# Inverse root of the mean squares on Pool by the power operation, in place of logarithm and exponentials on ScalarE

## The chip, the core and the metric

The kernel runs on one core of a Trainium2 chip. Its time is the device time of that core in microseconds (us). Before the change the median of three runs is 384.19 us (383.76 to 384.19). In the profile the engines are called PE (TensorE matmul; PEld is its weight load), DVE (VectorE), ACT (ScalarE), POOL (GpSimd, called Pool in this text) and SP (SyncE, which only issues transfers here).

## The reference

Attention comes first, over 8 batches of 12 heads with 448 tokens of 64 values. Every row of q and k is divided by the root of its mean square and multiplied by a gain, then comes softmax attention. Its output is the input of a layer of 8 experts, to which the tokens go by a hash of their identity. The first part is what the change touches:

```python
def rmsnorm(x, g):
    rms = np.sqrt(np.mean(x * x, axis=-1, keepdims=True) + 1e-06)
    return x / rms * g
q_n, k_n = (rmsnorm(q, g_q), rmsnorm(k, g_k))
scores = scale * np.matmul(q_n, k_n.transpose(0, 1, 3, 2))
attn = exp(scores - max); attn = attn / sum(attn)
attn_out = np.matmul(attn, v)
# then, for each expert e: out[mask] = np.maximum(x[mask] @ w1[e], 0.0) @ w2[e]
```

## The kernel before

The kernel has two stages, one after the other. The attention stage takes roughly the first 185 us, the expert stage the rest. In both, the instructions of every engine run in the order in which the program writes them (`tc.manual_schedule()`): an instruction that has to wait holds up everything behind it on the same engine.

**Steps and groups.** A step is one pair of heads; there are 48, six for each batch b. Steps are gathered into 17 groups g0 to g16, of three pairs each, but for the first two (one and two pairs). `s0[g]` is the first step of a group. Scores, exponentials and the product with v are done step by step. The norm of q and k is prepared for a whole group at a time, about three steps ahead.

**One step.** `score(s, j)` (L490 to L504) makes a block of scores on PE and its exponential on ACT (L498, and L503 for the last, smaller block). `transposes(s+1)` brings normalized q and k of the next step into the layout that the matmul needs, on PE (L475), and `transposed` evacuates them on DVE (L485 for kT, L487 for qT). `av_part(s-1, ...)` multiplies the exponentials of the step before with v on PE; at its end DVE takes the reciprocal of the row sums (L535) and multiplies (L536).

**The norm of a group**, which the change touches, has four parts.
1. `prep_sq` squares q or k (DVE, L275).
2. `prep_sum` and `prep_red` sum them up, on PE by matmuls with the identity (L287) and on DVE by a reduction (L295). The result is `ss`, the sums of squares: 128 partitions with 24 values for q and 24 for k.
3. `prep_rr` (L298 to L311) makes from `ss` the inverse root `rr`, on ACT: one logarithm (L303, in place, with the division by 64 and the epsilon), and two exponentials with the factor -0.5 (L305), one for q and one for k. The exponentials write each value twice, side by side, as 16-bit floats.
4. `prep_norm` (L313 to L323) multiplies q and k by `rr` in four instructions on DVE (L320). The results are what `transposes` reads.

**Where these stand.** From g3 on, `prep_rr` of group g is written at the end of step t = s0[g-1], and `prep_norm` of g in the middle of step t+1. Between the last reduction (L295) of a group and its `prep_norm`, DVE has only the rest of step t and the start of step t+1: L535, L536, L485, L487, and in the table steps also two small instructions of the routing table (L442).

**Pool's order.** Pool issues nearly all loads: q, k and v of later batches (`load_qk` and `load_v`, L230 to L240) and the expert weights (L156 for w1, L162 for w2, L816 in the expert stage). A load can be made to wait until an earlier load has landed, and then holds Pool's queue. Pool also sets up constants, clears buffers (L577, L580, L581, L599), and in the middle of the attention stage does part of the routing (L365 to L439) and 28 instructions `hi` (L444) of the routing table. At the end of the attention stage it starts the gathers (L173).

Of the kernel before, what the change touches and what calls it, by code (L numbers as in the profile page):

```python
# [8 lines left out]
FP32 = mybir.dt.float32  # L9
# [3 lines left out]
AF = mybir.ActivationFunctionType  # L13
ALU = mybir.AluOpType
# [5 lines left out]
def kernel(  # L20
# [12 lines left out]
    nc = tc.nc  # L33

    B, H, S, D = q.shape
# [3 lines left out]
    P = 128  # L39
# [5 lines left out]
    scale = 1.0 / float(D) ** 0.5  # L45
# [26 lines left out]
    consts = ctx.enter_context(tc.tile_pool(name="consts", bufs=1))  # L72
# [9 lines left out]

    tid32 = rt_keep.tile([P, NTC, 2], I32)
    gcol = consts.tile([P, 2], FP32)
    ident16 = consts.tile([P, P], FP16)
    u128 = consts.tile([P, P], BF16)
    ones128 = consts.tile([P, P], BF16)
    eps_col = consts.tile([P, 1], FP32)
# [110 lines left out]
    with tc.manual_schedule(), \  # L199
# [98 lines left out]
        def prep_rr(gi):  # L298
            n = groups[gi][2]
            ss = st[gi].pop("ss")  # L300
            m = 8 * n
            rr = a_st.tile([P, 2, 2, GMAX, 4, 2], FP16, name="rr")
            nc.scalar.activation(ss[:, :, 0:m], ss[:, :, 0:m], AF.Ln, bias=eps_col[:], scale=1.0 / D)  # L303
            for a in range(2):
                nc.scalar.activation(  # L305
                    rr[:, a, :, 0:n].rearrange("p hh n j t -> p n hh j t"),
                    ss[:, a, 0:m].rearrange("p (n hh j) -> p n hh j", hh=2, j=4)[
                        :, :, :, :, None].to_broadcast([P, n, 2, 4, 2]),
                    AF.Exp, bias=0.0, scale=-0.5)
            st[gi]["rr"] = rr  # L310
            st[gi]["n8"] = a_n8.tile([P, 2, GMAX, 4, 2, D], FP16, name="n8")  # L311
# [264 lines left out]
        def zero_q(eng, t, n0, n1):  # L576
            eng.memset(t[64:P, n0:n1, 3::4, :], 0.0)  # L577

        def zero_kv(eng, t, n0, n1):
            eng.memset(t[64:P, n0:n1, 3, :], 0.0)  # L580
            eng.memset(t[0:64, n0:n1, 7, :], 0.0)  # L581
# [8 lines left out]
        zero_kv(nc.vector, first[:, 1], 0, 1)  # L590
        zero_q(nc.vector, first[:, 0], 0, 1)
        nc.vector.memset(eps_col[:], 1e-6)
        zero_kv(nc.vector, k_bufs[0], 0, HP)
        zero_q(nc.vector, q_bufs[0], 0, HP)
        zero_kv(nc.vector, v_bufs[0], 0, HP)
# [18 lines left out]
        for a in (1, 0):  # L614
            prep_sq(0, a)
            prep_sum(0, a)
            spin(2)
            prep_red(0, a)
        prep_rr(0)
        spin(6)  # L620
        prep_sq(1, 1, True)
# [15 lines left out]
        prep_red(1, 0)  # L637
        score(0, 0)
        prep_rr(1)
        for j in (1, 2, 3):  # L640
            score(0, j)
# [19 lines left out]
        for g in range(1, NG):  # L661
            t = s0[g - 1]
            if g > 1:
                pre[t].append((prep_v, g))
            else:
                pre[1].append((prep_v, g))
            if g > 3:
                pre[s0[g - 2]].append((prep_sq, g, 1))
                mid[s0[g - 2] + 1].append((g, 1))
                pre[t - 1].append((prep_sq, g, 0))  # L670
                mid[t].append((g, 0))
            if g == 2:
                pre[1].append((prep_sq, 2, 0))
                mid[1] += [(2, 1), (2, 0)]
                post[1] += [(prep_rr, 2), (prep_norm, 2)]
            if g == 3:
                pre[2].append((prep_sq, 3, 1))
                mid[3] += [(3, 1), (3, 0)]
                pre[3].append((prep_sq, 3, 0))
            if g > 2:  # L680
                post[t].append((prep_rr, g))
                pre[t + 1].append((prep_norm, g))
        for s in range(1, NS):
            gi, i = steps[s]
            b, hp0, n = groups[gi]
# [226 lines left out]
```

## Time and profile before

The profile is of one execution with a span of 385.0 us. The table gives busy time in us by engine in four stretches of the span; a stretch's length is the most that one engine can be busy in it.

| stretch, us | PE | DVE | ACT | Pool | what runs |
|---|---|---|---|---|---|
| 0 to 50 (50) | 36.82 | 32.57 | 28.55 | 39.91 | first loads, norms of groups g0 to g4 |
| 50 to 100 (50) | 45.96 | 45.26 | 45.88 | 17.51 | attention, loads of later batches |
| 100 to 160 (60) | 57.69 | 58.97 | 56.04 | 29.12 | attention with the routing table |
| 160 to 180 (20) | 18.90 | 17.44 | 18.29 | 1.36 | last attention steps |
| 180 to 385 (205) | 185.16 | 61.76 | 38.73 | 87.17 | experts |

In such a table the engine with the least idle time in a stretch is the first candidate for what bounds it. In the expert stage this is PE alone. In the attention stage three engines are nearly full at once, so the waits of single instructions have to be read as well.

A page of the profile names groups of instructions by line, engine and operation, with the count, the busy time, the mean time of one in ns, and the idle time of the engine just ahead of them with what ended it. The timeline lists instructions in order of time: start, duration, engine, line, operation, output and input; the bracket at its end holds idle time and what ended it.

### The profile page before, as it was taken

The numbers are of one execution on the slowest core, as the hardware profiler recorded it, in microseconds if no ns is written. First come the engines' busy times: TensorE is split into PE (matmuls) and PEld (weight loads), VectorE is DVE, ScalarE is ACT, GpSimd is POOL, SyncE is SP. The second block draws the span as 40 slices with busy tenths as digits, with TensorE's granted clock in tenths as the row PEclk, the third lists the DMA queues.
The fourth block names the chain that finished last, engine by engine and source line by source line (L and its number), as shares of the span: only waits on it lengthen the run. The fifth ranks groups of instructions, "written<-read, shape, count | busy, mean of one in ns | idle before, by whom it ended". The sixth has DMA issues, their size and how long they took to land. (4 is left out here: it accounts for less than half of the span.)

```text
span 385.0 us, 9539 instructions
## 1 busy us (share of the span) xinstructions
PE 344.5 (89%) x4006; PEld 236.8 (62%) x4006; DVE 216.0 (56%) x519; ACT 187.5 (49%) x299; POOL 175.1 (45%) x247
## 2 busy tenths in 40 slices
PE   7755998989999999999899999999998989999960
PEld 3443776766766777776667666666665656666630
DVE  5674789989999999988633233333222322232210
ACT  3753899989899999989321112212021111212200
POOL 8998552014629950003347344462644636522030
PEclk9998899999999999999999999999999999999995
DMA  8999999943999999103548999999999999932030
GB/s 123 159 131 181 189 220 193 219 61 76 191 185 234 218 242 198 44 15 105 122 116 159 212 260 247 205 257 174 236 233 194 239 186 235 269 138 95 2 147 2
DMA packets 54269, 64.61 MB, mean 168 GB/s; under 512 B 22403, under 2 KB 42134, under 8 KB 53968
## 3 DMA queue, kind: packets, MB, share of 16 engines
q0 software_dynamic: 50592, 57.98, 85.8%
q1 hardware_dynamic: 3024, 5.41, 5.2%
q8 instruction: 32, 0.52, 0.6%
q10 hardware_dynamic: 608, 0.59, 0.5%
q14 instruction: 13, 0.11, 0.1%
HBM read 89.68 MB, written 18.09 MB: 280 GB/s over the span
## 5 line engine op out<-in xcount | busy, mean ns | idle before, releaser
L498 ACT ACTIVATE expT<-sc_ps 128x896 bf16<-128x896 f32 x144 | 123.9, 934 | 22.7 <-PE sc_ps L496 22.5
L765 PE MATMUL o_ps<-w_sb,h_sb 128*128 128x256 f16 (+1 forms) x512 | 87.9, 326 | 0.0
L752 PEld LDWEIGHTS <-w_sb 128*128 128x128 f16 x432 | 58.0, 144 | 25.7 <-issue 1.6
L752 PE MATMUL h_ps<-xT,w_sb 128*128 128x512 f16 x336 | 73.7, 379 | 0.0
L765 PEld LDWEIGHTS <-h_sb 128*128 128x128 f16 x512 | 48.9, 98 | 32.6
L173 POOL DMA_INDIRECT xg<-x_scratch,gidx x32 | 32.6, 1020 | 63.5 <-DVE x_sb L536 38.3
L770 POOL DMA_INDIRECT out_dram<-o_sb,gidx x32 | 33.0, 1031 | 51.5 <-ACT o_sb L769 17.0
L756 ACT ACTIVATE h_sb<-h_ps 128x512 f16<-128x512 f32 (+2 forms) x36 | 19.7, 550 | 75.1 <-PE h_ps L752 75.1
L758 DVE TENSOR_SCALAR h_sb<-h_ps 128x512 f16<-128x512 f32 (+2 forms) x36 | 22.8, 632 | 55.6 <-PE h_ps L752 55.6
L769 ACT COPY o_sb<-o_ps 128x768 f32<-128x768 f32 x16 | 12.8, 799 | 76.0 <-PE o_ps L765 51.3
L520 PEld LDWEIGHTS <-expT 128*128 128x128 bf16 x1152 | 42.5, 98 | 9.9 <-issue 6.0
L496 PE MATMUL sc_ps<-qT,kT 64*128 64x448 f16 x288 | 43.3, 358 | 4.5 <-DVE et L385 1.4
L520 PE MATMUL av_ps<-v,expT 128*128 128x65 bf16 x1152 | 44.0, 194 | 0.0
L769 DVE COPY o_sb<-o_ps 128x768 f32<-128x768 f32 x16 | 15.3, 958 | 45.7 <-PE o_ps L765 21.2
L816 POOL DMA_DIRECT2D w_sb<-in_moe_w_dram x36 | 23.1, 645 | 30.2 <-DMA w_sb<-in_moe_w_dram 28.2
L475 PE MATMUL qkT_ps<-ident,n 128*128 128x128 f16 x384 | 30.6, 222 | 5.4 <-DVE n L320 3.8
L475 PEld LDWEIGHTS <-n 128*128 128x128 f16 x384 | 22.3, 98 | 19.8 <-issue 11.9
L536 DVE TENSOR_TENSOR x_sb<-av_ps,srec 128x448 f16<-128x448 f32 x48 | 29.7, 619 | 1.5
L287 PEld LDWEIGHTS <-ident 128*128 128x128 f16 x544 | 24.6, 99 | 8.8 <-issue 6.8
L185 DVE COPY xT<-xT_ps 128x768 f16<-128x768 f16 x28 | 15.5, 554 | 23.9 <-PE xT_ps L184 23.8
L485 DVE TENSOR_SCALAR kT<-qkT_ps,g_col 128x512 f16<-128x512 f16 x48 | 23.1, 481 | 9.5 <-PE qkT_ps L475 8.4
L503 ACT ACTIVATE expT<-sc_ps 128x448 bf16<-128x448 f32 x48 | 27.7, 577 | 1.2 <-PE sc_ps L501 1.2
(140 smaller groups left out, 382.5 us busy)
## 6 DMA issues: line engine op xcount, KB each, us to landing
w_sb<-in_moe_w_dram POOLq DMA_DIRECT2D x32, 384.0 KB, 13.6
w_sb<-in_moe_w_dram POOLq DMA_DIRECT2D x12, 768.0 KB, 13.5
x_scratch<-x_sb SPq DMA_DIRECT2D x15, 288.0 KB, 6.1
w_sb<-in_moe_w_dram POOLq DMA_DIRECT2D x2, 1536.0 KB, 16.4
kr<-in_k_dram POOLq DMA_DIRECT2D x6, 384.0 KB, 9.0
qr<-in_q_dram POOLq DMA_DIRECT2D x3, 768.0 KB, 14.5
vr<-in_v_dram POOLq DMA_DIRECT2D x6, 384.0 KB, 19.4
kr<-in_k_dram POOLq DMA_DIRECT2D x6, 288.0 KB, 8.9
```

The costliest lines, as they stand in the source:

```text
L173: nc.gpsimd.indirect_dma_start(out=xg[:], out_offset=None, in_=x_dram[0:rows, :], in_offset=bass.IndirectOffsetOnAxis(ap=idx, axis=0), bou ...
L287: nc.tensor.matmul(sp, lhsT=ident16[:], rhs=sq[:, c, 0:m], start=(c == 0), stop=(c == NW - 1))
L475: nc.tensor.transpose(T[:, o:o + P], n8[:, a, i, j].rearrange("p h d -> p (h d)"), ident16[:])
L496: nc.tensor.matmul(sc[:, hh, :S], lhsT=kT[64 * hh:64 * hh + 64, P * j:P * j + P], rhs=qT[64 * hh:64 * hh + 64, :], start=True, stop=True)
L498: nc.scalar.activation(expT[:, 2 * j:2 * j + 2, :], sc[:, :, :S], AF.Exp, bias=0.0, scale=1.0)
L503: nc.scalar.activation(expT[:, 6, :], sc[:, 0, :S], AF.Exp, bias=0.0, scale=1.0)
L520: nc.tensor.matmul(av[:, 2 * t + hh, :], lhsT=expT[:, tl(hh, j), P * t:P * t + P], rhs=v8[:, i, 4 * hh + j, 0:D + 1], start=(j == 0), stop ...
L536: nc.vector.tensor_tensor(out=x_sb[:, :, hp * D:hp * D + D], in0=av[:, :, :D], in1=srec[:, :, None].to_broadcast([P, SL, D]), op=ALU.mult)
L752: nc.tensor.matmul(h_ps[:, :c1 - c0], lhsT=w1v[:, co, fo, :], rhs=xT[:, co, c0:c1], start=(co == 0), stop=(co == CO - 1))
L765: nc.tensor.matmul(o_ps[:, d0:d1], lhsT=h_sb[:, fo, col * P:(col + 1) * P], rhs=w2_sb[:, fo, d0:d1], start=(fo == 0), stop=(fo == FO - 1))
L769: (nc.vector.tensor_copy if col % 2 else nc.scalar.copy)(o_sb[:], o_ps[:])
L770: scat = nc.gpsimd.indirect_dma_start(out=out[:, :], out_offset=bass.IndirectOffsetOnAxis(ap=idx, axis=0), in_=o_sb[:], in_offset=None, bo ...
```

## The change

From group g3 on (`gi > 2`), `prep_rr` is done by four instructions of Pool in place of three of ACT: a multiply and add for the mean and the epsilon, a power with the exponent -0.5, which is read from a new constant column `mhalf`, and two copies that write each value twice as 16-bit floats. Groups g0 to g2 keep the logarithm and the exponentials on ACT. The change is meant to take work from ACT, which also makes all exponentials of the softmax, and to put it on an engine with more idle time.

```diff
+    mhalf = consts.tile([P, 1], FP32)
...
-            nc.scalar.activation(ss[:, :, 0:m], ss[:, :, 0:m], AF.Ln, bias=eps_col[:], scale=1.0 / D)
+            on_pool = gi > 2
+            if on_pool:
+                nc.gpsimd.tensor_scalar(out=ss[:, :, 0:m], in0=ss[:, :, 0:m], scalar1=1.0 / D,
+                                        scalar2=1e-6, op0=ALU.mult, op1=ALU.add)
+                nc.gpsimd.tensor_tensor(out=ss[:, :, 0:m], in0=ss[:, :, 0:m],
+                                        in1=mhalf[:, :, None].to_broadcast([P, 2, m]), op=ALU.pow)
+            else:
+                nc.scalar.activation(ss[:, :, 0:m], ss[:, :, 0:m], AF.Ln, bias=eps_col[:],
+                                     scale=1.0 / D)
             for a in range(2):
+                if on_pool:
+                    nc.gpsimd.tensor_copy(
+                        rr[:, a, :, 0:n].rearrange("p hh n j t -> p n hh j t"),
+                        ss[:, a, 0:m].rearrange("p (n hh j) -> p n hh j", hh=2, j=4)[
+                            :, :, :, :, None].to_broadcast([P, n, 2, 4, 2]))
+                    continue
                 nc.scalar.activation(
                     rr[:, a, :, 0:n].rearrange("p hh n j t -> p n hh j t"),
...
         nc.vector.memset(eps_col[:], 1e-6)
+        nc.vector.memset(mhalf[:], -0.5)
```

## The prediction

> **What bounds the kernel now.** I read the page's table of slices first, to see which engine is full where.
>
> ```profile
> PE   7755998989999999999899999999998989999960
> DVE  5674789989999999988633233333222322232210
> ACT  3753899989899999989321112212021111212200
> POOL 8998552014629950003347344462644636522030
> ```
>
> The change acts only in the attention stage, slices 5 to 19. PE, DVE and ACT are all nearly full there, so no engine can simply be called the bound. The busy times by stretch separate them: from 100 to 160 us DVE is busy 58.97 of 60 us, ACT 56.04, PE 57.69; from 50 to 100 us DVE 45.26 of 50, ACT 45.88. So between 100 and 160 DVE is the bound and ACT has 4 us to spare; between 50 and 100 neither has much. From 180 us on PE is busy 185 of 205 us, and the expert stage can't start before the last scores: a delay of attention is a delay of the end.
>
> Next the groups that the change removes, kept apart by shape.
>
> ```profile
> L305 ACT ACTIVATE rr<-ss 128x48 f16<-128x48 f32 x30 | 5.6, 234 | 0.5
> L303 ACT ACTIVATE ss<-ss,eps_col 128x48 f32<-128x48 f32 x15 | 4.9, 326 | 0.1
> ```
>
> Then the timeline of DVE around one norm (g4), for the time that a replacement has.
>
> ```profile
> 48.74 0.25 DVE L295 TENSOR_REDUCE ss<-qkT_ps 128x24 f32<-128x96 f32 x1
> 48.91 0.20 DVE L535 RECIPROCAL srec<-av_ps 128x7 f32<-128x7 f32 x1
> 49.14 0.62 DVE L536 TENSOR_TENSOR x_sb<-av_ps,srec 128x448 f16<-128x448 f32 x1
> 49.91 0.48 DVE L485 TENSOR_SCALAR kT<-qkT_ps,g_col 128x512 f16<-128x512 f16 x1
> 50.31 0.38 DVE L487 COPY qT<-qkT_ps 128x448 f16<-128x448 f16 x1
> 50.62 1.03 DVE L320 TENSOR_TENSOR n<-kr,rr 128x768 f16<-128x768 f16 x2
> ```
>
> The sums are ready at 48.99, and the norm starts at 50.62 with no idle time ahead of it. The inverse root has 1.63 us in which it costs nothing: I call this the slack. The same two lines of the other groups give g3 3.00, g5 1.39, g6 1.63, g7 2.09, g8 1.63, g9 1.68, g10 2.24, g11 1.90, g12 1.73, g13 1.70, g14 1.70, g15 2.68, g16 1.92.
>
> Last the timeline of Pool, for what stands ahead of the new instructions.
>
> ```profile
> 43.49 0.73 POOL L581 MEMSET vr<- 64x768 bf16 x1
> 52.19 2.98 POOL L240 DMA_DIRECT2D kr<-in_k_dram  x4 [7.96 <-ACT expT L498]
> ...
> 62.35 0.74 POOL L240 DMA_DIRECT2D vr<-in_v_dram  x1 [1.15 <-DMA kr<-in_k_dram]
> ...
> 101.61 0.75 POOL L240 DMA_DIRECT2D vr<-in_v_dram  x1 [0.86 <-DMA kr<-in_k_dram]
> ...
> 114.14 0.62 POOL L156 DMA_DIRECT2D w_sb<-in_moe_w_dram  x1 [3.02 <-DMA qr<-in_q_dram]
> ```
>
> Pool is no free engine: it clears buffers until 44.22, and its loads wait until earlier loads land, until 63.09, 102.36 and 114.76.
>
> [...] L240 sat 7.96 us and nothing behind it ran. [...] L320 took 0.51 us apiece at 40.26, under Pool's memsets, and 0.51 at 50.62 without. [...]
>
> **The change part by part.**
>
> *Removed from ACT*: 14 groups (g3 to g16). From L303 to the next exponential ACT takes 0.63 us (38.73 to 39.36), so 14 x 0.63 = 8.8 us. This is worth time only where ACT ends last; behind a DVE that waits longer it is worth nothing.
>
> *Added to DVE*: one memset of 128x1 at the start, about 0.1 us by Pool's row of that size (99 ns), among waits for the first loads: nothing. DVE's later work is the same, with a wait on Pool in place of one on ACT.
>
> *Added to Pool*: per group a multiply-add, a power, two copies, all 128x48 or halves, each waiting for the one before.
> - Multiply-add: L388, 128x8, 194 ns; with 40 more elements 0.25.
> - Copies to 16 bits, 48 outputs each: the cast L138 to 16 bits, 128x128, took 640 ns; the smallest casts 186. In between by size 0.36, less if the two overlap: 0.3 each, 0.6.
> - Gaps between dependent Pool instructions: 84.66 to 84.75, 0.1 each; with the hand-over from and to DVE 0.4.
> - Power: not in the trace. Lower bound from L444, a program of two operations with a column operand: 570 ns at its fastest for 64 elements, against 309 for the same kind with 8 (L392), so 4.7 ns an element; 0.2 + 48 x 0.0047 = 0.4 us. [...] I take 2.2 us, [...]; no trace or run decides it yet.
>
> So the chain c = 0.25 + 0.6 + 0.4 + 2.2, about 3.4 us; with the bounds 1.65 and 6.25.
>
> *Ten groups with Pool free* (g4, g6, g7, g8, g11 to g16): their slacks sum to 18.6 us. DVE stands still for 10 x 3.4 - 18.6 = 15.4 us. Behind the waiting L320 on DVE are the next reduction, L535 and L536 (which free av_ps for PE) and the next kT and qT (which PE's scores, and so ACT, need), so the whole pipeline stops. DVE can win back only idle time: its waits from 50 to 178 us sum to 5.7; I take half, 2.8. Cost 12.6.
>
> *g3*: in the changed instruction order its four Pool instructions stand behind all memsets, so they start at 44.22, and rr comes at 44.22 + 3.3 = 47.5 instead of by 40.26. Stall 7.3, less DVE's two waits on PE just after (0.36 and 0.63): 6.3.
>
> *g5*: behind the v loads, whose last issue ended at 63.09 (or some 61.3, if these land as fast as the batch from 93 us, which took 9.1 us for the same issues). rr comes at 64.6 to 66.4 instead of 61.26: 3.3 to 5.1, I take 4.0.
>
> *g9*: behind the last v load, ended 102.36: rr at 105.7 instead of 102.34, 3.3.
>
> *g10*: behind w1's four issues, 21.5 us after the batch of loads began (93.25), while the norm came 19.5 after (112.77). g9's stall has already moved the norm by 3.3, so what is left is 21.5 + 3.3 - 19.5 - 3.3 = 2.0, whatever c is.
>
> *Pool's other work*: the `hi` instructions and three weight loads now stand between waits for sums, so they run later. The last weight load moves from 139 to about 163 us plus the shift; it lands 16.4 us after issue by its row, ahead of its use in the second expert. Nothing.
>
> Sum: 12.6 + 6.3 + 4.0 + 3.3 + 2.0 = 28.2. Predicted 384.2 + 28.2 = 412.4, say 412.
>
> **The rivals.**
> 1. *Short power* (0.4 us, c = 1.65): the ten free groups fit in their slack, and only the groups behind Pool's queue pay: g3 4.5, g5 2.4, g9 1.6, g10 2.0, 10.5; less idle time won back, 2.8. 384.2 + 7.7 = 392. For it: a short row such as L444. Against it: the power is many times L444's two operations.
> 2. *Long power* (5.0 us, c = 6.25): free groups 62.5 - 18.6 - 2.8 = 41.1, g3 9.1, g5 6.8, g9 6.2, g10 2.0: 65.2, so 449. [...]
> 3. *ACT was the bound* (faster): if Pool's chain were hidden in every group and ACT ended each step, up to 8.8 us would come off, 375. For it: between 50 and 100 us ACT is busiest by a hair. Against it: DVE's 58.97 of 60, and g3, which can't be hidden whatever the power costs: the memsets end 4 us after the norm of before.
>
> **How the numbers follow.** Main case 0.50 (412), short power 0.22 (392), long power 0.23 (449 and beyond), ACT bound 0.05 (375). The range should leave 2 in 10 out: from just under the short case, 390, to just over the long case, 452. Faster only by the last rival, 0.05; within 0.2% needs the short power and more relief of ACT than I see, 0.02; slower 0.93.
>
> **What would show it.** Right: four Pool lines in `prep_rr`, 14 or 28 times each, with the power near 2 us; idle time on DVE ahead of L320, ended by Pool's rr, longest at g3 (about 7 us) and above 3 at g5 and g9; the last L320 some 28 us later than 174 us; the expert stage as long as before. Wrong: a power of a few tenths of a us, or DVE idle elsewhere. If the expert stage grew, the weight loads that I costed at nothing were not hidden. What I can least bound is the power: each us of it moves the result by some 13 us.

## The result, and the profile after

The changed kernel takes 505.25 us (median of four runs, 502.80 to 505.62); the kernel before took 383.98 us beside it. The ratio is 1.3155 with a 95% interval of 1.3102 to 1.3208: 121 us slower. The forecast was 412 us with a range of 390 to 452, so the direction was right and the size far too small.

The page of the kernel after, busy time in 40 slices of 12.5 us, and the clock granted to TensorE:

```profile
PE   8662547647745745845845858999999999999990
DVE  4660634634734744843754555433232323233210
ACT  3744346345536436436535634221211111211210
POOL 9879289265399486697877380553465545353120
PEclk9987678778779679679859879999999999999996
```

Between slices 3 and 23 none of PE, DVE and ACT stays full any more. They go up and down together, where in the attention stage they were mostly at 8 or 9 before, and Pool reaches 9 in only five of these slices. Engines that idle together may be waiting for one common thing. The clock differs too. In the page of the kernel before it was

```profile
PEclk9998899999999999999999999999999999999995
```

and after the change it goes between 5 and 9 in these slices, mostly from 6 to 8, and returns to 9 when the expert stage begins.

The costliest groups of the page after the change name the common thing (line, engine and operation, shapes, count, busy time, mean ns, then the idle time ahead and what ended it). Line numbers are those of the changed file; L335 was L320 before:

```profile
L308 POOL TENSOR_TENSOR ss<-ss,mhalf 128x48 f32<-128x48 f32 x14 | 112.3, 8023 | 1.2
...
L335 DVE TENSOR_TENSOR n<-kr,rr 128x768 f16<-128x768 f16 (+1 forms) x32 | 16.2, 546 | 107.2 <-POOL rr L315 105.4
...
L306 POOL TENSOR_SCALAR ss<-ss 128x48 f32<-128x48 f32 x14 | 3.2, 232 | 59.9 <-DVE ss L296 41.4
```

One power takes 8.02 us, where the prediction took 2.2, and 5.0 in its long rival. DVE sat idle for 105.4 us in all ahead of the norm, in each of the 14 groups until Pool's rr was there. The multiply-add is as short as forecast, 0.23 us.

One of the 14 stalls (g8) in the timeline of the kernel after, cut to the chain; the bracket of the last line is the stall:

```profile
136.07 0.25 DVE L296 TENSOR_REDUCE ss<-qkT_ps 128x24 f32<-128x96 f32 x1
...
136.42 0.24 POOL L306 TENSOR_SCALAR ss<-ss 128x48 f32<-128x48 f32 x1 [2.86 <-DVE ss L296]
...
136.74 8.03 POOL L308 TENSOR_TENSOR ss<-ss,mhalf 128x48 f32<-128x48 f32 x1
...
137.65 0.38 DVE L502 COPY qT<-qkT_ps 128x448 f16<-128x448 f16 x1
...
144.83 0.39 POOL L315 CAST rr<-ss 128x48 f16<-128x48 f32 x2
...
145.25 1.03 DVE L335 TENSOR_TENSOR n<-kr,rr 128x768 f16<-128x768 f16 x2 [7.22 <-POOL rr L315]
```

The chain from the end of the reduction (136.32) to the norm (145.25) is 8.93 us: the power 8.03, everything else together 0.9. DVE has done its other work by 138.03 and waits. PE and ACT soon run dry as well, because what stands behind the norm on DVE is what they need next.

The waits of DVE between 36 and 297 us, the stretch of the 14 norms, sum as follows (waiting line, what it waited for, us in total, times, longest; the four largest):

```profile
DVE n L335 <- POOL rr L315: 105.4, 14, 14.3
DVE kT L500 <- PE qkT_ps L490: 11.7, 20, 1.3
DVE srec L550 <- PE av_ps L542: 6.3, 14, 0.8
DVE ss L296 <- PE qkT_ps L288: 1.4, 2, 0.9
```

Before, between 36 and 178 us, the second was 5.8 and the third did not occur. So 105.4 us are the direct stalls, and 12.2 (5.9 + 6.3) are more waiting on PE. Together they are 117.6 us, beside the 119.2 us by which the last norm starts later (291.97 against 172.79). The expert stage takes no longer than it did: from its first weight load on PE to the end of the span 193.2 us (308.0 to 501.2), before 196.9 (188.1 to 385.0).

### The profile page after: what moved, and what is told of

The parts are those of the page before. It is cut to its first block, busy times and chain, and to the rows that moved or that the text cites. A ratio compares the mean times of both kernels' runs of the same rounds, so it can differ in the third digit from the quotient of the medians.

```text
span 501.2 us, 9570 instructions
## 1 busy us (share of the span) xinstructions
PE 364.2 (73%) x4006; PEld 252.8 (50%) x4006; DVE 219.8 (44%) x520; ACT 182.8 (36%) x257; POOL 298.6 (60%) x303
## 5 line engine op out<-in xcount | busy, mean ns | idle before, releaser
L513 ACT ACTIVATE expT<-sc_ps 128x896 bf16<-128x896 f32 x144 | 122.2, 922 | 55.1 <-PE sc_ps L511 55.1
L490 PE MATMUL qkT_ps<-ident,n 128*128 128x128 f16 x384 | 38.2, 256 | 104.8 <-DVE ss L296 94.4
L308 POOL TENSOR_TENSOR ss<-ss,mhalf 128x48 f32<-128x48 f32 x14 | 112.3, 8023 | 1.2
L490 PEld LDWEIGHTS <-n 128*128 128x128 f16 x384 | 28.8, 114 | 126.3 <-DVE n L335 98.6
L335 DVE TENSOR_TENSOR n<-kr,rr 128x768 f16<-128x768 f16 (+1 forms) x32 | 16.2, 546 | 107.2 <-POOL rr L315 105.4
L535 PEld LDWEIGHTS <-expT 128*128 128x128 bf16 x1152 | 52.3, 110 | 12.5 <-issue 9.7
L535 PE MATMUL av_ps<-v,expT 128*128 128x65 bf16 x1152 | 53.5, 211 | 0.0
L306 POOL TENSOR_SCALAR ss<-ss 128x48 f32<-128x48 f32 x14 | 3.2, 232 | 59.9 <-DVE ss L296 41.4
```

The lines of the kernel that those rows point to most:

```text
L308: nc.gpsimd.tensor_tensor(out=ss[:, :, 0:m], in0=ss[:, :, 0:m], in1=mhalf[:, :, None].to_broadcast([P, 2, m]), op=ALU.pow)
L490: nc.tensor.transpose(T[:, o:o + P], n8[:, a, i, j].rearrange("p h d -> p (h d)"), ident16[:])
L513: nc.scalar.activation(expT[:, 2 * j:2 * j + 2, :], sc[:, :, :S], AF.Exp, bias=0.0, scale=1.0)
L535: nc.tensor.matmul(av[:, 2 * t + hh, :], lhsT=expT[:, tl(hh, j), P * t:P * t + P], rhs=v8[:, i, 4 * hh + j, 0:D + 1], start=(j == 0), stop ...
```

## The experiments

The theory to test is that the power's own duration, which stands between the sums and the norm on DVE, makes the time. The first rival is that moving the work to Pool, with its queue and hand-overs, makes it. The smaller question is where the further waits on PE come from. The runs fell on more than one chip, and the kernel before took 384 to 391 us there, so each is set against the kernel before beside it. Diffs are against the changed kernel.

### The same on Pool, without the power (e1_mult)

```diff
-                     in1=mhalf[:, :, None].to_broadcast([P, 2, m]), op=ALU.pow)
+                     in1=mhalf[:, :, None].to_broadcast([P, 2, m]), op=ALU.mult)
```

> The power on Pool is replaced by a product of the same two operands, so the inverse root is left out and everything else, engine, order and waits, is that of the changed kernel. Theory A, the power's own 8.02 us is what costs: the chain falls from 8.96 to about 1.2 us, below every slack but those behind Pool's queue (g3 some 4, g5 1 to 3, g9 1, g10 2), so about 392 us (386 to 396). Rival B, the move to Pool itself costs (hand-overs, Pool's queue): above 440 us.

Measured: 396.26 us against 384.58, ratio 1.0306 (1.0215 to 1.0396), just above the 386 to 396 us of theory A and far from the 440 of rival B. 109 of the 121 us are gone. The product takes 267 ns on Pool where the power took 8023, with the same operands, so neither their shape nor the column operand makes the price. Four waits on Pool are left; the timeline of DVE in this run shows them as:

```profile
46.04 1.03 DVE L335 TENSOR_TENSOR n<-kr,rr 128x768 f16<-128x768 f16 x2 [5.45 <-POOL rr L315]
...
69.33 1.03 DVE L335 TENSOR_TENSOR n<-kr,rr 128x768 f16<-128x768 f16 x2 [2.35 <-POOL rr L315]
...
110.51 1.03 DVE L335 TENSOR_TENSOR n<-kr,rr 128x768 f16<-128x768 f16 x2 [1.04 <-POOL rr L315]
...
123.14 1.03 DVE L335 TENSOR_TENSOR n<-kr,rr 128x768 f16<-128x768 f16 x2 [2.10 <-POOL rr L315]
```

They are g3, g5, g9 and g10, the four groups that stand behind the clearing of buffers and behind loads on Pool. In the ten others the norm does not wait for Pool: the short chain fits in their slack. The rival is refuted in the main, but Pool's queue has a share of some 11 us. And ACT, relieved of 14 logarithms and 28 exponentials as in the changed kernel, gave nothing back that the time shows: the kernel took 11.7 us longer, with 10.9 us of waits.

### Half the power (e2_half)

```diff
-                nc.gpsimd.tensor_tensor(out=ss[:, :, 0:m], in0=ss[:, :, 0:m],
-                                        in1=mhalf[:, :, None].to_broadcast([P, 2, m]), op=ALU.pow)
+                nc.gpsimd.tensor_tensor(out=ss[:, 1, 0:m], in0=ss[:, 1, 0:m],
+                                        in1=mhalf[:].to_broadcast([P, m]), op=ALU.pow)
```

> The power is done for k alone, 24 values a partition in place of 48; for q the root is left out and the mean square itself is used. If the power costs by the element (8.02 / 48 = 0.167 us each, nothing fixed): 4.0 us, chain 4.95; stalls: ten free groups 49.5 - 18.6 = 31, g3 8.9, g5 and g9 3.7 more than with the product (6.0 and 4.7), g10 2: 53 us, so 437 us, or 445 if every us of stall costs 1.15 us as in the changed kernel (121.3 over 105.4). If the power has a large fixed part: near 500 us.

Measured: 450.37 against 390.36 us, ratio 1.1519 (1.1452 to 1.1587), 60.0 us more. The power's group in the profile of this run:

```profile
L308 POOL TENSOR_TENSOR ss<-ss,mhalf 128x24 f32<-128x24 f32 x14 | 58.5, 4178 | 1.2
```

and DVE's wait for Pool, summed over the run:

```profile
DVE n L335 <- POOL rr L315: 51.0, 14, 10.4
```

From these two lengths the power costs by the element of a partition: (8023 - 4178) / 24 = 160 ns each, and 0.33 us fixed. The stalls, 51.0 us, had been forecast at 53 by the sum of chains less slacks, with a power of 4.0 us in it. As in the changed kernel the time grew by more than the stalls, by a factor of 60.0 / 51.0 = 1.18 (there 121.3 / 105.4 = 1.15). The absolute time lies above the 437 to 445 us of the forecast because the kernel before took 390 us on this chip.

### One group at a time (e3_only_g12, e3_only_g10, e3_only_g3)

```diff
-            on_pool = gi > 2
+            on_pool = gi == 12      # e3_only_g12; 10 and 3 in the two others
```

> Only group g12 has its inverse root on Pool, where Pool is otherwise free. Theory A (stall = chain less slack): 8.96 - 1.73 = 7.2 us, so 391 us, and 392.5 if one stall also lowers PE's granted clock as much as a fourteenth of the 16 us that the 14 stalls leave unexplained. Rival C, the 14 stalls feed each other and a single one is mostly won back: under 387 us.

> Only group g10 has its inverse root on Pool, behind the four issues of expert weights that ended at 114.76 us in the kernel before. If Pool's queue delays it as I predicted: rr at 114.76 + 8.9 = 123.7 instead of 112.77, stall 10.9, so 395 to 396 us. If the queue costs nothing: 8.96 - 2.24 = 6.7, so 391 us.

> Only group g3 has its inverse root on Pool, behind the clearing of buffers that ended at 44.22 us. If the queue delays it: 44.22 + 8.9 - 40.26 = 12.9 us, less up to 2 won back, so 395 to 397 us. If the queue costs nothing: 8.96 - 3.00 = 6.0, so 390 us.

The one wait of each run, in the sums of DVE's waits, for g12:

```profile
DVE n L335 <- POOL rr L315: 7.2, 1, 7.2
```

for g10:

```profile
DVE n L335 <- POOL rr L315: 10.8, 1, 10.8
```

and for g3:

```profile
DVE n L335 <- POOL rr L315: 13.1, 1, 13.1
```

All three are what chain, slack and Pool's queue give: 7.2, 10.9 and 12.9 were expected. The times, all against 384.58 us: 395.02 (ratio 1.0278, 1.0219 to 1.0337), 396.35 (1.0296, 1.0236 to 1.0355) and 398.73 (1.0382, 1.0320 to 1.0444), so 10.4, 11.8 and 14.2 us more. For g12 the time grew by 3.2 us more than its stall, over what I had allowed, and the two others ended slightly above their ranges too; the ratios are uncertain by some 2 us, so I read no more from them than that no stall was won back. That g10 alone waits 10.8 us, and only 6.58 as one of fourteen, shows the part of the queue. Alone, g10's multiply-add had to stand behind the last of Pool's weight issues, which ended at 116.00. In the changed kernel these issues had ended at 167.50 and the sums of g10 came only at 173.68, so the queue cost nothing more.

### PE kept busy during the stalls (e4_warm, e9_again, e8_warm12)

The granted clock was 0.77 from 40 to 297 us in the changed kernel, 0.99 from 40 to 190 us before. I added matmuls on zeros in one step of each group, where PE waits for the norm:

```diff
+        fill = [s0[g - 1] + 2 for g in range(3, NG)]
...
             score(s, 2)
+            if s in fill:
+                T = ps_sc.tile([P, 2, 512], FP32, name="sc_ps")[:, 0]
+                for _ in range(26):
+                    nc.tensor.matmul(T[:, 0:448], lhsT=warm[:, 0:P], rhs=warm[:, 0:448],
+                                     start=True, stop=True)
             if nxt:
                 transposes(s + 1)
```

> The changed kernel with 26 matmuls on zeros added where PE waits in each of the 14 stalls, so that PE isn't idle there; the result doesn't use them. Theory T (what the stalls don't explain, 121.3 - 105.4 = 16 us, is PE's lower granted clock after idle stretches, 0.77 between 40 and 297 us): the clock stays near 1 and about 16 us come back, 489 us (485 to 495). Rival U (the 16 us are the refilling of the pipeline after each stall, at any clock): 503 to 508 us, with the clock up.

Measured: 507.50 against 390.36 us, ratio 1.2994 (1.2911 to 1.3077). The time of this run decides nothing, for in two groups, g7 and g8, the added work ran at the wrong time. From the timeline of this run at g7:

```profile
124.90 0.17 PE L395 MATMUL sc_ps<-oc,emask 128*128 128x8 bf16 x1 [5.22 <-POOL oc L387]
...
126.59 7.56 PE L710 MATMUL sc_ps<-warm 128*128 128x448 f16 x26 [0.63 <-ACT expT L513]
...
134.63 0.48 DVE L500 TENSOR_SCALAR kT<-qkT_ps,g_col 128x512 f16<-128x512 f16 x1 [6.50 <-PE qkT_ps L490]
```

PE waited there for `oc`, a small cast of the routing that stands behind the power on Pool, and did the 26 matmuls after the stall, at DVE's cost (6.5 us at g7 and 7.5 at g8). The wait for `oc` is in the changed kernel too, 5.1 us, hidden under the stall. Outside these two groups DVE's waits on PE for kT and srec came to 5.0 us, against 18.0 in the changed kernel (11.7 + 6.3), with a granted clock of 0.943 over the whole execution, where the changed kernel had 0.868. So I left out these two groups, took 20 matmuls, and ran the changed kernel again on the same chip.

```diff
+        fill = [s0[g - 1] + 2 for g in range(3, NG) if g not in (7, 8)]
...
+                for _ in range(20):
```

> The changed kernel once more, unaltered, so that e8 can be set against it on the same chip: 1.31 to 1.32 times the kernel before.

> As e4 with 20 matmuls on zeros instead of 26, and none after g7 and g8, where in e4 PE's queue stood behind the routing's wait for Pool and the added matmuls ran only after the stall (6.5 and 7.5 us of waits of their own). Theory T (PE's lower granted clock after idle stretches makes up what the stalls don't explain): waits of DVE on PE for kT and srec fall from 15.3 and 8.6 us to below 9 together, and the time is 10 to 16 us below e9. Rival U (refilling of the pipeline at any clock): within 4 us of e9.

Measured: e9 507.09 us (ratio 1.2948, 1.2878 to 1.3017), e8 501.56 us (1.2802, 1.2728 to 1.2877), both against 391.12. The ratio of e9 is below the 1.31 to 1.32 that I had expected: the kernel before was slower on this chip than in the first comparison, by 7 us, and the changed kernel by only 2. DVE's two waits on PE from 36 to 297 us, in e9:

```profile
DVE kT L500 <- PE qkT_ps L490: 12.7, 20, 1.3
DVE srec L550 <- PE av_ps L542: 5.3, 13, 0.6
```

and in e8, where the granted clock in that stretch was 0.90 instead of 0.77:

```profile
DVE kT L500 <- PE qkT_ps L490: 7.7, 13, 1.3
DVE srec L550 <- PE av_ps L542: 3.2, 7, 0.6
```

The waits went from 18.0 to 10.9 us, not quite below 9. The time fell by 5.5 us, which lies between the forecasts of the two theories; the intervals of the two ratios do not overlap (1.2878 and 1.2877 are their near ends), nor do the single runs (505.69 and more against 503.04 and less). In the two profiled executions the stretch from the norm of g3 to that of g16 is 8.4 us shorter in e8 (230.7 against 239.1 us). The stalls themselves were nearly equal (104.9 and 106.0). So a part of what the stalls leave over goes with PE's clock, which was higher when PE was kept busy; that it is all of it is not shown.

### The power out of the way (e5_early_pool, e6_early_act)

If the power is expensive only because of its place, it must cost nothing where there is time for it. For g7, g8, g15 and g16 q's squares and sums are made three steps earlier, and the root by halves as soon as a half has its sums; the other groups stay on ACT. In e6 the same halves are done on ACT. (`half_rr` is `prep_rr` for one half; `d` is 3 for these groups and 0 for the others.)

```diff
+        EARLY_G = (7, 8, 15, 16)
+        ROOT_ON_POOL = True      # e5; False in e6
...
-                pre[t - 1].append((prep_sq, g, 0))
-                mid[t].append((g, 0))
+                if not d:
+                    pre[t - 1].append((prep_sq, g, 0))
+                    mid[t].append((g, 0))
+                elif g - 1 in EARLY_G:
+                    pre[t - 4].append((prep_sq, g, 0))
+                    mid[t - 3].append((g, 0))
+                    post[t - 3].append((half_rr, g, 0))
+                else:
+                    pre[t - 4].append((prep_sq, g, 0, False, "sq_k"))
+                    post[t - 4] += [(prep_sum, g, 0), (prep_red, g, 0), (half_rr, g, 0)]
+                if d:
+                    post[t - 2].append((half_rr, g, 1))
```

> Groups g7, g8, g15 and g16 alone have the root on Pool, by halves (k and q apart), and the squares and sums of q are made three steps earlier, so that q's chain has some four steps and k's some two and a half (7.8 us) for about 4.9 us each; all other groups stay on ACT. If the cost was only that the power stood in the slack: no wait of DVE on Pool, and 382 to 385 us, with at most 4 x 0.63 = 2.5 us won from ACT. If a long power on Pool slows DVE [...]: DVE's squares and norms last longer than 0.95 and 0.51 us, and 386 us or more.

> The control of e5: the same earlier squares and sums of q for g7, g8, g15 and g16 and the same halves, but logarithm and exponentials on ACT, two short ones of each more. If the earlier order costs nothing: 384 to 386 us, and e5 less than this by 0 to 2.5 us.

Measured, both against 390.36 us: e5 399.37 (ratio 1.0230, 1.0180 to 1.0280), e6 392.30 (1.0073, 1.0046 to 1.0101). e6 is some 2 us slower than the kernel before, so the earlier order seems to have a small cost of its own, and e5 is not the faster of the two, as the first theory required. No norm waits for Pool's rr in e5, so the chain is hidden as intended, and still the median is 7.1 us above that of e6. The profile of e5 shows where time may go, from the waits of DVE

```profile
DVE emp L494 <- PE sc_ps L490: 3.1, 1, 3.1
...
DVE t L434 <- POOL hole L433: 2.4, 1, 2.4
```

and of PE:

```profile
PE sc_ps L420 <- POOL oc L412: 1.3, 1, 1.3
```

All three belong to the routing, whose small Pool instructions (`oc`, `hole`, and for L494 the last `hi`) now stand behind a power of 4.2 us. The first is 0.3 us in e6, and the two others don't occur there, so these waits are 6.5 us longer than in e6. The medians differ by 7.1 us, but the spans of the two profiled executions only by 4.5 (396.2 against 391.7). The waits are thus large enough to make the difference; that they add up one to one is not shown. DVE's instructions were no slower: the squares took 0.95 us and the norm's 0.55, as in e6. So the slower DVE of the other theory is not the cause, though e5's time falls where that theory had put it.

### The power with nothing behind it (e10_g16_early, e11_g16_early_act)

Now only g16 is made early, after the routing is done, on Pool and on ACT. The rest of the edit is that of e5, but the root of q comes one step later.

```diff
+        EARLY_G = (16,)
+        ROOT_ON_POOL = True      # e10; False in e11
```

> Only g16 has its root on Pool, made early and by halves as in e5, at a place where Pool has nothing else to do and no routing work waits behind it. If e5's extra time over e6 is the routing's wait behind the power on Pool (oc 1.3, hole 2.4, the routing table 3.1 us), nothing of it is left here: same as the kernel before within 0.5% (ratio 0.995 to 1.005), though the power takes two times 4.2 us. If a power on Pool costs by itself [...]: 4 to 8 us more than before.

> The control of e10: g16's root in the same place, in the same halves, with the same earlier squares and sums, but by logarithm and exponentials on ACT. If the 0.7% of e10 comes from the earlier order: 1.004 to 1.010 times the kernel before, as e10. If it comes from the power on Pool, though hidden: 0.998 to 1.003.

Measured: e10 393.54 against 391.12 us, ratio 1.0070 (1.0044 to 1.0096); e11 395.17 against 390.84, ratio 1.0117 (1.0071 to 1.0162). e10 is just outside what I had set as equal, but its control is no faster. Had the 7.1 us of e5 been the price of four such roots on Pool in themselves, one of them would have put e10 some 1.8 us, or 0.45%, above e11; it is 0.47% below, with an uncertainty of about 0.5% (the two ran on different chips, each against the kernel before). So the small loss goes with the earlier order, as in e6, and a power on Pool that nothing waits for cost nothing that these runs can tell. No version came out ahead of the kernel before.

## Why the prediction was wrong

- **The term that failed is the power, 2.2 us an instruction in the main case and 5.0 in the long rival.** It took 8.02, and so the chain 8.93 us instead of 3.4. Both figures were my own estimates, and no trace or run had shown either: the rows of L444 and L392 gave the short case alone. Measured are 160 ns an element. That it is "many times L444's two operations" was right: 8.02 us for 48 elements, against a mean of 0.75 us for L444's 64. The mechanism was right: DVE waited for Pool's rr at every norm, and e1 and e2 show that the length of the power set these waits. The long-power rival came nearest, but its value too was short. Putting 8.0 into my own sum, whose slope was 13 us for each us of power, gives 28.2 + 13 x 5.8 = 104 us, so 488: the rest of the sum was off by 17 us of 121.
- **Slack and chain held.** The ten groups with Pool free: 10 x 8.93 - 18.6 = 70.7 us of stall by the working, 69.3 measured. The parts of the chain other than the power came out smaller, 0.9 us instead of 1.2.
- **Pool's queue held where it was alone.** Without the power the four waits were 5.45, 2.35, 1.04 and 2.10 us, forecast in the short-power rival as 5.5 (4.5 after winning back), 2.4, 1.6 and 2.0. The rival's 0.4 us happens to lie near the product's 0.27, which stood for the power in that run. With long stalls g10's fixed 2.0, "whatever c is", was wrong: it waited 6.58, because the norm had moved beyond Pool's weight issues and it became a group like the others. g3 waited 14.3, g5 7.4 and g9 7.9.
- **"DVE can win back 2.8 us" and 1.0 after g3: wrong sign.** Nothing was won back. DVE's waits on PE grew by 12.2 us instead. When PE was kept busy during the stalls, a part of these went away (7.1 us of waits, 5.5 us of time) while the clock rose.
- **That the relief of ACT, 8.8 us, is worth nothing behind a waiting DVE: right**, and by e1 it was worth nothing that shows even without the power. One point given for the rival *ACT was the bound* was misread: between 50 and 100 us PE was the busiest by a hair (45.96 us), not ACT (45.88).
- **The weight loads at no cost: right**; the expert stage is no longer. But *"Pool's other work: nothing"* was incomplete. The routing's small Pool instructions stand behind the power as well; in the changed kernel their wait hides under the stalls (PE's 5.1 us for `oc`), and in e5 such waits were 6.5 us longer than in e6.

## What to carry to other kernels

Before work goes to an engine with idle time, ask what waits for its answer and how long that may take: here there were 1.4 to 2.7 us of slack in most groups against a chain of 8.9, fourteen times. When the price of an operation isn't known, an assumed count of steps is no bound, and the range must then be open at that end. And what stands behind a long instruction on its engine waits with it: in e5 no norm waited for the power of 4.2 us, and still the waits for the routing's small instructions behind it were 6.5 us longer than in e6. Hiding the long instruction itself is not enough when small ones behind it are waited for.

## What the runs showed of the hardware that I had not expected

- The power on Pool (two fp32 operands, 128 partitions): 4178 ns for 24 elements a partition, 8023 for 48, so 160 ns an element; the product of the same operands took 267 ns for 48. Starts agree with the length: in the stall shown above Pool's next instruction begins 8.09 us after the power.
- A power on Pool did not hold up DVE in e5. Two pairs of norms (L360, two SBUF inputs) ran at 82.15 and 83.09 us for 1.02 us a pair, under a power from 80.51 to 84.67; in the kernel before, a pair took 1.03 at 50.62, with no instruction on Pool.
- One multiply-add of Pool in e5 took 0.85 us, where the others took 0.21 to 0.24: at 161.69, while DVE made squares (161.52 to 162.47). What made it longer is not shown.
- In the changed kernel, where PE waited 94.4 us in 13 stretches ahead of L490, the granted clock was 0.77 from 40 to 297 us, against 0.99 from 40 to 190 us before. With matmuls on zeros in twelve of the fourteen stalls (e8) it was 0.90 from 36 to 297 us, against 0.77 in e9 beside it.
